# Moving a dense layer's row loads, row products and weight narrowing between queues and engines

## The chip, the cores and the metric

The kernel runs on one core of a Trainium2 chip. The metric is device time in microseconds (us) from one launch; it is read as the median of several runs. The engines are named as in the profile: PE is TensorE (matmuls), PEld its weight load, DVE is VectorE, ACT is ScalarE, POOL is GpSimd, SP is SyncE, which here only issues DMAs.

## What is computed

Three parts follow each other: attention with a bias that a small network makes of positions, a dense layer of two matrix products with a leaky activation, and a mixture of experts. Only the seam between the first two and the dense layer itself matter here. Cut to that:

```python
attn_out = attn @ v                      # softmax(q k^T / 8 + bias), 4 x 8 heads, 576 rows, 64 wide
x = attn_out.transpose(0, 2, 1, 3).reshape(2304, 512)
h = x @ w_in                             # 512 -> 2048
g = np.maximum(h, 0.0) + alpha * np.minimum(h, 0.0)
y = g @ w_out                            # 2048 -> 512; goes into the routing and the experts
```

## The kernel before, in words

**Attention** works through 16 pairs (two heads of one batch entry each) in rounds; an instruction list (ROUND) fixes the order, and nearly every instruction is pinned to it. Of each pair it writes the unnormalised output, transposed, to a DRAM tensor xT, and the inverse row sums to a DRAM tensor rs.

**The dense layer** cuts its 2304 rows into 6 blocks of 384 and the hidden width into 16 pieces f of 128. One step is one block and one f. A step's `up` is 12 matmuls of 384 columns that make h, then two ScalarE passes (L699, L701), one VectorE pass (L702) that makes g, a ScalarE pass that makes its high part gh (L709) and one that makes its low part gl (L711; GpSimd for block 0, VectorE for the others). Its `down` is 9 matmuls of 512 columns that add into three PSUM tiles ys. The loop issues `up` of step n+1 ahead of `down` of step n. Blocks 0 and 1 are interleaved and share their weights (steps n = 0 to 31: block 0's f and, two f behind, block 1's); blocks 2 to 5 follow one by one. All products use a high and a low part of each operand, so every operand passes through a cast to its high part on ScalarE and a subtraction for its low part.

**Weights.** The 16 pieces arrive as 64-bit numbers, 1 MB each (w_fetch, w_load: tile `wide`). `w_narrow` makes 32-bit ones of them by three VectorE passes (L649, L650, L651; tile `wr`), and then starts the load of piece f+2. `w_split` makes high and low parts (tiles w0h, w0l and so on, numbered on through the blocks: w16 is block 2's first, w32 block 3's, w48 block 4's); the low part L680 is VectorE's or GpSimd's by the list WL_DVE. Pieces 0 and 1 are narrowed in slices inside attention's fixed order. Piece 2 is fetched by a hook in the last full round but one of attention and narrowed by a call of w_narrow behind attention's code. `prep(n + 3)` does narrowing and splitting three steps ahead of use.

**Rows.** For a block's 384 rows, each of four column groups c needs xT's rows (tile xa, or xs for block 2) and rs spread over 64 partitions twice (tile rb): `x_load` issues three DMAs. Then VectorE multiplies the two (L587, `x_sum`), ScalarE casts to the high part (L592) and VectorE subtracts for the low part (L593). rb has one buffer, xa two. Blocks 0 and 1 go another way, inside attention (`x_early`, on GpSimd, L604 to L606). Block 2's rows are loaded and made in one go near the end of blocks 0 and 1, those of blocks 3 to 5 at f = 4, 6, 8 and 10 of the block before.

**Order.** A scheduler orders each engine's instructions by a simulated time in which transfers have a modelled duration; an instruction whose operands it takes to be ready may move ahead of others of its engine. `keep_in_program_order(i)` ties i behind the instruction of the same engine that was traced just before it, and to nothing else. Each engine, and SP's queue, runs its instructions strictly in the order that comes out.

**Routing.** When a block ends, its ys are copied out by ScalarE (L763) and VectorE (L764, tile y) and routed during the next block, a piece after each step; blocks 2 to 5 share one set of ys tiles.

## Time and profile before

| | |
|---|---|
| runs | 848.19, 850.45, 856.14 us; median 850.45 us |
| profiled execution | 855.61 us, of which the span from first to last instruction is 853.4 us |
| busy share of the span | PE 91%, PEld 76%, DVE 66%, ACT 57%, POOL 36% |
| chain that ended last | PE 42% of the span, DVE 3%, DMA 3%, ACT 2% |
| dense layer, about 319 to 778 us | PE busy but for short stretches; its granted clock is full (1.00) except behind some of them |

The busy share counts all time in which an instruction was in progress. An engine's clock is given as the share of full speed that was granted (1.00 is 2.4 GHz, 0.50 is 1.2 GHz); only PE's changes here. What costs time in a kernel with a PE this busy is read from stretches of 20 us: how much of each PE was idle, and how much it ran at the lower level.

### The profile page before, as it was taken

How to read it: one execution, taken by the hardware profiler on the slowest of the kernel's cores; microseconds unless marked ns; L12 is line 12 of the kernel's file. 1: busy time of each engine (PE TensorE's matmuls, PEld its weight loads, DVE VectorE, ACT ScalarE, POOL GpSimd, SP SyncE). 2: the span in 40 equal slices, each digit the busy share in tenths (PEclk: the TensorE clock that was granted, in tenths of full speed). 3: DMA queues.
4: the chain of work that ended last, by engine and by line, in shares of the span. 5: the costliest groups of instructions: out<-in, count | busy, mean ns of one | idle time of the engine just before them, and what ended most of it. 6: DMA issues, size and time to landing. Idle time of an engine off the chain costs nothing.

```text
span 853.4 us, 18376 instructions
## 1 busy us (share of the span) xinstructions
PE 780.0 (91%) x7428; PEld 647.7 (76%) x7428; DVE 561.1 (66%) x979; ACT 485.7 (57%) x961; POOL 304.8 (36%) x231
## 2 busy tenths in 40 slices
PE   5876599999999898999999999989989999998994
PEld 5766577777777667898998789879878899886332
DVE  8956668888888758897336665755666656465103
ACT  8742478888888744334446555646554656554002
POOL 6974325365564613114221431433233232131000
PEclk9989799999999999999999999999989999999897
DMA  6799895948742424553002000410010014337996
GB/s 204 183 211 194 192 243 174 249 119 233 239 133 85 143 91 164 197 201 119 2 1 65 10 1 1 160 38 1 1 28 1 1 58 154 109 104 263 391 379 222
DMA packets 59493, 114.44 MB, mean 134 GB/s; under 512 B 10640, under 2 KB 38160, under 8 KB 57360
## 3 DMA queue, kind: packets, MB, share of 16 engines
q1 hardware_dynamic: 59408, 113.26, 44.0%
q8 instruction: 58, 0.95, 0.5%
q14 instruction: 27, 0.22, 0.1%
HBM read 91.95 MB, written 21.29 MB: 133 GB/s over the span
## 4 chain that ended last, share of the span: by engine, by line
PE 42%; DVE 3%; DMA 3%; ACT 2%; issue 1%; POOL 0%; SPq 0%; DVEq 0%; ACTq 0%
PE ys L723 17%; PE h L691 16%; PE ops L1091 3%; DMA rb<-rs 2%; PE hps L1091 2%; DVE xa L587 1%; PE lp L783 1%; DMA xa<-xT 1%; PE turn L1100 0%; PE o L1118 0%; PE tl L830 0%; DVE g L702 0%; ACT g L699 0%; PE sp L842 0%; PE sp L843 0%
## 5 line engine op out<-in xcount | busy, mean ns | idle before, releaser
L702 DVE SCALAR_TENSOR_TENSOR g<-g,nal 128x384 f32<-128x384 f32 x96 | 87.7, 913 | 76.3 <-ACT g L701 75.8
L419 ACT ACTIVATE e<-z,m 128x576 f32<-128x576 f32 x144 | 109.9, 767 | 22.0 <-DVE m L399 22.0
L399 DVE CUSTOM_DVE_ANT_0 z<-s,nb 128x576 f32<-128x576 f32 x144 | 108.2, 755 | 18.7 <-PE s L381 11.0
L709 ACT ACTIVATE gr<-g 128x384 fp32r<-128x384 f32 x95 | 49.8, 524 | 113.1 <-DVE g L702 113.0
L467 PE MATMUL o<-g,v 128*64 128x256 f32 (+1 forms) x640 | 88.9, 424 | 4.1 <-DVE m L399 3.6
L455 ACT ACTIVATE g<-t 128x640 f32<-128x640 f32 x96 | 67.2, 702 | 34.7 <-PE t L439 30.7
L161 PE MATMUL acc<-wp,mask 128*128 128x64 bf16 (+1 forms) x1680 | 59.2, 201 | 22.1 <-issue 12.5
L161 PEld LDWEIGHTS <-mask 128*128 128x128 bf16 (+1 forms) x1680 | 57.0, 105 | 24.1 <-issue 14.7
L439 PE MATMUL t<-ident,e 64*128 64x64 f32 x1440 | 68.7, 224 | 5.8 <-DVE m L399 3.6
L711 DVE TENSOR_TENSOR gr<-g,gr 128x384 fp32r<-128x384 f32 x79 | 53.4, 676 | 31.4 <-ACT gr L709 29.7
L439 PEld LDWEIGHTS t<-ident,e 64*128 64x128 f32 x1440 | 66.2, 140 | 7.7 <-issue 5.4
L699 ACT ACTIVATE g<-h 128x384 f32<-128x384 f32 x96 | 46.7, 486 | 43.9 <-PE h L691 41.5
L467 PEld LDWEIGHTS o<-g,v 128*64 128x64 f32 x640 | 44.8, 141 | 34.0 <-DVE m L399 3.8
L381 PE MATMUL s<-kh,qh 64*128 64x288 f32 x320 | 62.0, 383 | 8.1 <-DVE rows L186 5.6
L142 ACT ACTIVATE mask<-pr,wb 128x576 bf16<-128x576 f16 (+4 forms) x81 | 47.0, 665 | 24.1 <-PE acc L161 24.1
L711 POOL TENSOR_TENSOR gr<-g,gr 128x384 fp32r<-128x384 f32 x16 | 20.0, 1250 | 93.2 <-ACT gr L709 78.4
L381 PE MATMUL s<-kh,ql 64*128 64x288 f32 x320 | 48.8, 299 | 0.0
L381 PE MATMUL s<-kl,qh 64*128 64x288 f32 x320 | 48.8, 300 | 0.0
L354 POOL TENSOR_SCALAR qh<-raw 128x1216 fp32r<-128x1216 f32 x16 | 19.4, 1210 | 80.2 <-PE s L381 75.5
L701 ACT ACTIVATE g<-h 128x384 f32<-128x384 f32 x96 | 46.6, 486 | 0.0
L381 PEld LDWEIGHTS s<-kh,qh 64*128 64x128 f32 x320 | 31.7, 193 | 17.2 <-issue 7.6
L356 POOL TENSOR_TENSOR ql<-raw,qh 128x1216 fp32r<-128x1216 f32 x16 | 44.7, 2793 | 0.0
(986 smaller groups left out, 2048.4 us busy)
## 6 DMA issues: line engine op xcount, KB each, us to landing
wide<-in_w_dram SPq DMA_DIRECT2D x16, 1024.0 KB
ep<-in_mw_dram SPq DMA_DIRECT2D x30, 512.0 KB
raw<-in_qk_dram SPq DMA_DIRECT2D x16, 896.0 KB
nb<-W SPq DMA_DIRECT2D x12, 576.0 KB
v<-in_v_l_dram SPq DMA_DIRECT2D x16, 320.0 KB
pre<-in_mw_dram SPq DMA_DIRECT2D x10, 512.0 KB
er<-in_mw_dram SPq DMA_DIRECT2D x9, 512.0 KB
em<-in_mw_dram SPq DMA_DIRECT2D x8, 512.0 KB
```

What stands on the lines that cost most here:

```text
L161: nc.tensor.matmul(dst[:, u // 8, :, :, 4 * (u % 8) : 4 * (u % 8) + 4], mask[:, (16 * k + u) % RING, cols], wp[:, part], start=part == 0, ...
L381: nc.tensor.matmul(s[:, hf, :288], st["q", a][d, o : o + P], st["k", b][d, 288 * h : 288 * h + 288], start=n_ == 0, stop=n_ == len(seq) - 1,),
L399: self.nc.vector.tensor_tensor_reduce(out=z.rearrange("p (a b) -> p a b", a=2), in0=s[:, :, :288], in1=self.nb[st["hp"]][:, slot].rearrang ...
L419: self.nc.scalar.activation(e, z, AF.Exp, bias=m, scale=-1.0, accum_out=st["sum"][:, slot : slot + 1]),
L439: self.pin(i, nc.tensor.transpose(tp[:, r, 64 * c : 64 * c + 64], e[q, k0 : k0 + P], self.ident[q, q]))
L455: self.pin(i, nc.scalar.activation(dst, src, AF.Copy))
L467: nc.tensor.matmul(op[64 * h : 64 * h + 64, 0, :n], st["v"][:, h, c], g[:, h, c], start=c == 0, stop=c == 4),
L691: nc.tensor.matmul(h, w_[:, c * P : (c + 1) * P], x_[:, c], start=c == 0 and n_ == 0, stop=c == NC - 1 and n_ == 2,)
L702: nc.vector.scalar_tensor_tensor(g, neg, self.nal[:, f : f + 1], g, ALU.mult, ALU.add)
L709: nc.scalar.activation(gh, g, AF.Copy)
L711: eng.tensor_tensor(gl, g, gh.bitcast(F32), ALU.subtract)
L723: i = self.nc.tensor.matmul(self.ys[blk][t], g_[:, t * P : (t + 1) * P], w_[:, 512:], start=f == 0 and n_ == 0, stop=f == NF - 1 and n_ == 2,)
```

## The change

Four edits, all in the dense layer and its seam with attention.

- **Rows of blocks 3 to 5**: loads stay at f = 4, 6, 8 and 10; product, cast and low part are traced one step later, at f = 5, 7, 9 and 11. Product and low part go to GpSimd, each tied behind the instruction traced before it on that engine. As rb has one buffer, the load of group c+1 follows the product of group c, and so stands two steps ahead of its own product.
- **Rows of block 2**: loads stay; product, cast and low part of groups 0 and 1 are traced one step later, of groups 2 and 3 two steps later. Products go to GpSimd, tied; low parts stay on VectorE, tied.
- **Narrowing**: the first of the three VectorE passes is tied behind the VectorE instruction traced before it; the other two depend on it. For piece 2 that puts it behind attention's last VectorE instruction.
- **Fetch of piece 2**: its hook moves from the eighth to the fourth transpose of the same round.

```diff
@@ class Moe
-    def x_sum(self, xu, rb):
-        self.nc.vector.tensor_tensor(xu, xu, rb, ALU.mult)
-
-    def x_split(self, blk, c, xu):
-        nc = self.nc
-        xh, xl = self.x[blk]
-        nc.scalar.activation(xh[:, c], xu, AF.Copy)
-        nc.vector.tensor_tensor(xl[:, c], xu, xh[:, c].bitcast(F32), ALU.subtract)
...
-    def x_make(self, blk, c, xu, rb):
-        self.x_sum(xu, rb)
-        self.x_split(blk, c, xu)
-
+    def x_make(self, blk, c, xu, rb, low):
+
+        nc = self.nc
+        xh, xl = self.x[blk]
+        self.tc.keep_in_program_order(nc.gpsimd.tensor_tensor(xu, xu, rb, ALU.mult))
+        nc.scalar.activation(xh[:, c], xu, AF.Copy)
+        self.tc.keep_in_program_order(low.tensor_tensor(xl[:, c], xu, xh[:, c].bitcast(F32), ALU.subtract))
...
@@ w_narrow
-        nc.vector.tensor_scalar(t, w[:, :, 1], 3, 0x3FFFFFFF, ALU.logical_shift_left, ALU.bitwise_and)
+        i = nc.vector.tensor_scalar(t, w[:, :, 1], 3, 0x3FFFFFFF, ALU.logical_shift_left, ALU.bitwise_and)
+        self.tc.keep_in_program_order(i)
...
@@ run
                 for c in range(NC):
                     self.x_load(2, c, *x2[c])
-                for c in range(NC):
-                    self.x_sum(*x2[c])
                 self.x_alloc(2)
-                for c in range(NC):
-                    self.x_split(2, c, x2[c][0])
+            for k in range(2):
+                if n + 1 < total and seq[n + 1] == (1, NF - 2 + k):
+                    for c in (2 * k, 2 * k + 1):
+                        self.x_make(2, c, *x2[c], nc.vector)
             if n < total - LATE_DOWN:
                 self.down(n, us.pop(n))
             elif n == total - 1:
                 break
-            if 2 <= blk < NBLK - 1 and 4 <= f < 12 and f % 2 == 0:
+            if 2 <= blk < NBLK - 1 and 4 <= f < 12:
                 c = (f - 4) // 2
-                if c == 0:
+                if f == 4:
                     self.x_alloc(blk + 1)
-                t3 = parts(c, blk + 1)
-                self.x_load(blk + 1, c, *t3)
-                self.x_make(blk + 1, c, *t3)
+                if f % 2 == 0:
+                    t3 = parts(c, blk + 1)
+                    self.x_load(blk + 1, c, *t3)
+                else:
+                    self.x_make(blk + 1, c, *t3, nc.gpsimd)
...
-        at(i - np_, 7, moe.w_fetch, f)
+        at(i - np_, 3 if f == 2 else 7, moe.w_fetch, f)
```

## Rows read from the trace of the kernel before

**Rows 1.** Busy time by stretch of 20 us (in brackets instructions), then PE's clock, DMA share, GB/s

```profile
core 0: us, PE busy (x) PEld busy (x) DVE busy (x) ACT busy (x) POOL busy (x), PEclk, DMA share, GB/s
280.00:300.00 20.00, 16.37 (x205) 11.77 (x201) 15.46 (x34) 13.17 (x29) 12.34 (x11) 0.86 0.42 133
...
340.00:360.00 20.00, 18.23 (x85) 15.95 (x84) 17.77 (x20) 6.55 (x14) 2.58 (x2) 0.91 0.58 200
...
400.00:420.00 20.00, 19.75 (x98) 17.75 (x99) 6.36 (x9) 9.72 (x19) 5.44 (x4) 1.00 0.01 2
...
460.00:480.00 20.00, 18.09 (x88) 15.27 (x87) 12.28 (x17) 11.19 (x21) 5.58 (x3) 0.91 0.15 48
...
560.00:580.00 20.00, 16.98 (x90) 15.38 (x90) 10.59 (x13) 7.98 (x14) 8.15 (x4) 0.91 0.08 20
...
620.00:640.00 20.00, 15.76 (x76) 14.00 (x75) 13.71 (x18) 11.10 (x22) 6.90 (x4) 0.83 0.11 30
```

**Rows 2.** PE's timeline: start, duration, instruction, in brackets idle time before and its releaser

```profile
295.79 4.53 PE L467 MATMUL o<-g,v 128*64 128x256 f32 x20 [3.63 <-DVE m L399]
...
355.67 0.53 PE L723 MATMUL ys<-w2h,gr 128*128 128x512 f32 x1 [1.77 <-ACT gr L709]
...
456.06 0.50 PE L691 MATMUL h<-x,w16h 128*128 128x384 f32 x2
...
471.74 0.60 PE L770 MATMUL ty_0th<-idr,y 128*128 128x128 f32 x4 [1.83 <-DVE y L764]
...
563.03 0.96 PE L723 MATMUL ys<-w34h,gr 128*128 128x512 f32 x3 [3.02 <-DVE gr L711]
...
633.26 0.80 PE L723 MATMUL ys<-w48h,gr 128*128 128x512 f32 x1 [4.24 <-DVE y L764]
```

**Rows 3.** DVE's timeline at the end of attention

```profile
287.69 1.42 DVE L641 SCALAR_TENSOR_TENSOR wr<-wide,wr 128x512 uint32<-128x512 uint32 x1
...
294.37 0.69 DVE L649 TENSOR_SCALAR wr<-wide 128x1024 uint32<-128x1024 uint32 x1 [3.24 <-DMA wide<-in_w_dram]
```

**Rows 4.** SP's timeline at the end of attention

```profile
289.13 0.33 SPq L623 DMA_DIRECT2D wide<-in_w_dram  x1
```

**Rows 5.** DVE's timeline in blocks 2 to 4

```profile
465.68 0.56 DVE L587 TENSOR_TENSOR xa<-xa,rb 128x384 f32<-128x384 f32 x1 [3.20 <-DMA rb<-rs]
...
469.93 0.56 DVE L587 TENSOR_TENSOR xa<-xa,rb 128x384 f32<-128x384 f32 x1 [1.19 <-DMA rb<-rs]
...
558.61 2.76 DVE L587 TENSOR_TENSOR xa<-xa,rb 128x384 f32<-128x384 f32 x1 [2.30 <-DMA rb<-rs]
...
619.74 2.11 DVE L702 SCALAR_TENSOR_TENSOR g<-g,nal 128x384 f32<-128x384 f32 x1 [1.15 <-ACT g L701]
...
630.03 2.57 DVE L587 TENSOR_TENSOR xa<-xa,rb 128x384 f32<-128x384 f32 x1 [2.07 <-DMA rb<-rs]
```

**Rows 6.** POOL's timeline in the dense layer

```profile
451.67 1.26 POOL L711 TENSOR_TENSOR gr<-g,gr 128x384 fp32r<-128x384 f32 x1 [8.20 <-ACT gr L709]
...
619.03 2.41 POOL L680 TENSOR_TENSOR w49l<-wr,w49h 128x1024 fp32r<-128x1024 f32 x1 [2.00 <-ACT w49h L678]
```

**Rows 7.** Groups by line, 318 to 790 us: busy us, mean ns of one

```profile
L702 DVE SCALAR_TENSOR_TENSOR g<-g,nal 128x384 f32<-128x384 f32 x96 | 87.7, 913 | 76.3 <-ACT g L701 75.8
L711 DVE TENSOR_TENSOR gr<-g,gr 128x384 fp32r<-128x384 f32 x79 | 53.4, 676 | 31.4 <-ACT gr L709 29.7 <-issue 1.3
...
L699 ACT ACTIVATE g<-h 128x384 f32<-128x384 f32 x96 | 46.7, 486 | 43.9 <-PE h L691 41.5 <-DVE gr L711 1.4 <-POOL gr L711 1.0
...
L651 DVE SCALAR_TENSOR_TENSOR wr<-wide,wr 128x1024 uint32<-128x1024 uint32 x13 | 18.0, 1388 | 0.1
```

**Rows 8.** Line 604's instructions: duration in ns, least, median, most

```profile
L604 POOL TENSOR_TENSOR xu<-xu,xb x8: 1004/1010/1531, 131.6 to 298.8; 128x384 f32<-128x384 f32 x8
```

**Rows 9.** The chain that ended last, 415 to 430 us: start, us, what

```profile
417.08 2.09 PE ys L723 x9
419.17 2.08 PE h L691 x12
```

**Rows 10.** ACT's timeline in block 2

```profile
461.79 1.04 ACT L678 ACTIVATE w18h<-wr 128x1024 fp32r<-128x1024 f32 x1
```

## Prediction

> **What bounds the kernel now.** I read three views, in this order. First the busy time in stretches of 20 us, to see where PE loses time at all [rows 1]. The stretch from 400 us is what a good one looks like: PE busy for 19.75 of 20 us at full clock. A step of the dense layer there is nine matmuls of a `down` and twelve of an `up`, 2.09 + 2.08 = 4.17 us [rows 9]. Five stretches fall short, and each loses twice: PE idles, and behind the idle time it runs for some microseconds at the lower of its two clocks, where a matmul takes twice as long. I count the idle time as 20 less the busy time, and the clock as 20 x (1 - PEclk).
>
> Second, PE's own timeline, for who ended each long idle time; third, the timelines of the engines so named. All five come down to one pattern: a VectorE instruction that waits for a DMA, or has work in front of it that waits for one, with everything behind it in VectorE's strict order, although that work was ready.
>
> At 291 us PE waits 3.63 us for attention's score pass [rows 2]. That pass stands in VectorE's queue behind the first narrowing pass of piece 2, which waited 3.24 us for its weights [rows 3]. These were asked for only at 289.13 [rows 4], just as the last slice of piece 1, which used the same buffer, ended at 289.11 [rows 3]. Nothing needs piece 2 before the dense layer; the scheduler took its weights as landed.
>
> At 471 us PE waits 1.83 us for a copy of ys, at 563 us 3.02 us for a low part of g, at 633 us 4.24 us for a copy of ys again [rows 2]. In front of these stand row products that waited 3.20 and 1.19 us, 2.30 us, and 2.07 us for the inverse sums rb [rows 5]. These products belong to the next block, or the one after; with one rb buffer each could ask for its sums only when the one before was done, and each was placed early. Two of them took 2.76 and 2.57 us in place of 0.56 [rows 5].
>
> At 355 us PE waits 1.77 us for a cast of g [rows 2]: VectorE is busy for 17.77 us of that stretch, but for 6.36 of the one from 400 us [rows 1]. It narrows weights far ahead of use, and g queues between.
>
> **The change, part by part.**
>
> *Narrowing of piece 2.* Its first pass is tied behind attention's last VectorE instruction, so it can't stand in front of a score pass. This returns 3.63 us of idle time and 20 x 0.14 = 2.8 us of clock [rows 1, 2]: **6.4 us**. The fetch three transposes earlier in its round gives nothing: the transfer still waits for the buffer until 289.11, and SP has little to hold back there. The three passes (0.69 us [rows 3] and two of at most 1.39 [rows 7]) now fall behind attention, 3.5 us, while PE has three `up` of pieces 0 and 1 (6.2 us by [rows 9]) to do; if that cover were gone they would cost up to 3.5.
>
> *Narrowing of the others.* Tied behind the low part of g of the step before, VectorE's work spreads. The idle time at 355 us goes, with its clock: 1.77 + 1.8 = **3.6 us** [rows 1]. The tie has its price. The piece's `up` comes two `up` and three `down` behind the `up` whose low part now precedes the narrowing: five half-steps, 10.4 us [rows 9]. Into these must go three ScalarE passes of 0.49, g 0.91 and its low part 0.68 [rows 7], narrowing 0.69 + 2 x 1.39 [rows 3, 7], a cast of 1.04 [rows 10] and, where GpSimd makes the weight's low part, 2.41 [rows 6]. That is 9.97 us, with 0.4 to spare; one more g in between, and it is 0.5 late. Five of the fourteen pieces have their low part on GpSimd, one of them piece 2. The others save about half of 2.41, and are in time. So the cost lies between 0 and 4 us (four pieces, 1 us each); I take 1.0, as PE has other matmuls to fill with. The load of piece f+2 follows the narrowing of f and then has two steps of 4.17 us twice over, 16.7 us, against some 5 us from 289.13 to 294.37 [rows 3, 4]: it isn't late.
>
> *Rows of blocks 3 to 5.* Twelve products and twelve low parts leave VectorE, and with them the waits for rb. This returns what PE lost at the three block boundaries, by [rows 1]: 1.91 + 1.8, 3.02 + 1.8 and 4.24 + 3.4, **16.2 us**. On GpSimd the product stands behind the weight's low part of the step, two steps (8.3 us) behind its load; the waits of 1 to 3 us above end inside that. If one doesn't, only weight low parts are queued behind it on GpSimd, made three steps ahead. ScalarE's cast, which isn't tied, may wait for the product with relus behind it; that is in the bounds below. Next late after the DMA waits is the copying out of ys at a boundary: blocks 2 to 5 share these tiles, so the first `down` waits for three copies whatever the change does. I leave 1.0 us of the boundaries unrecovered (0 to 3).
>
> *What GpSimd costs VectorE.* A product takes 1.01 us there [rows 8] against 0.56 [rows 5], hidden as GpSimd is idle for most of each stretch [rows 1]. What isn't hidden is that VectorE stands still: the g pass from 619.74 took 2.11 us and ended 0.4 us behind GpSimd's pass from 619.03 to 621.44 [rows 5, 6]. The mean g takes 0.91 and the mean low part 0.68 [rows 7], where a product of that size alone takes 0.56 [rows 5]: at most 96 x 0.35 + 79 x 0.12 = 43 us of delay, from 125 us of GpSimd work in the layer (43 weight low parts of 2.4, 16 low parts of g of 1.3 [rows 6]), 0.34 us for each. The 28 new passes (16 products, 12 low parts) of 1.01 us make 28 us, so 9.6 us of delay, in pieces of less than 1 us. On the path I take 1.5 us, with 0 and 9.6 as ends, as a step fills 4.17 us of PE and the path of a step's g 3 us (below).
>
> The Trainium skill speaks against this part: "GPSIMD Engine Reference", section "Engine selection", gives plain elementwise work to VectorE, as GpSimd takes about twice as long with two inputs. "SBUF — State Buffer" (section "SBUF: two separate sides") adds that the two share a port pair as an exclusive lock. The rows agree with both; counted as that lock at its worst, all 28 us would come back as cost and the gain would be near nothing, which is rival 1 at its end.
>
> *Rows of block 2.* Their products move from VectorE, where they were placed early, to GpSimd behind the low part of g that starts at 451.67 [rows 6]; four of 1.01 us end at about 457. The low parts of groups 2 and 3 stand behind g's low part of the last step before block 2, 3.05 us behind that `up` (three ScalarE passes of 0.49, g 0.91, low part 0.68 [rows 7]), and end 1.1 us later at 4.2, with up to 1 us more if a GpSimd pass is in the way. Block 2's first `up`, which began at 456.06 [rows 2], follows one `down` and wants the last of them at its tenth matmul, 2.09 + 1.7 = 3.8 us behind [rows 9]. So 0.4 to 1.4 us late, unless PE does the next `down` first; with copies of ys on VectorE in between it could be 4. I take 1.0 (0 to 4).
>
> **The sum.** Gains 6.4 + 3.6 + 16.2 = 26.2 us; costs 1.0 + 1.0 + 1.5 + 1.0 = 4.5; net 21.7. The profiled execution took 855.61 us, 5.2 above the median; the order of instructions that causes the stalls is the same in each execution, so the difference holds for both: 855.61 - 21.7 = 833.9 for such an execution, and 850.45 - 21.7 = **828.8 us** as the forecast for the median.
>
> **Rivals.** *1. GpSimd holds VectorE on the path.* For: 0.3 us of delay for each us already. Against: it moves short pieces, and a step has slack. At 9.6 us of delay in place of 1.5, and as much again for the clock, it costs 16.2 more: 845. If all 28 us came onto the path, the time would be 828.8 - 1.5 + 28 = 855, no measurable gain. *2. The stalls only change place.* The change would not do what it says: boundaries stay as the copying of ys, not the DMA wait, ends them. For: PE's releaser at 471 and 633 is that copy. Against: in all three places the DMA wait stands right before it. With half of 16.2 kept as loss: 837. *3. Slower: weights late.* If the tied narrowing misses its `up` by 1.8 us, which it does once the 10 us above become more than 12.2, each of 13 pieces costs what the stall at 355 us did, 3.6 us: 47 - 26 = 21 us, 871. Against: two thirds of the pieces have a margin above 1 us, and PE can do other matmuls.
>
> **How the numbers follow.** Forecast 0.73, rival 1 (845 to 855) 0.12, rival 2 0.10, rival 3 0.05. With all costs at zero the time would be 824, and single runs before lie 2 below to 6 above their median: low end 817. The costs at their upper ends (boundaries 3, late weights 4, GpSimd 9.6, block 2's rows 4: 20.6 in place of 4.5) would give 845; few will be there at once, and 842 leaves out rivals 1 and 3, 0.17. Within 1% (8.5 us) is about what a measurement can't tell from no change. Forecast, rival 2 and a little of rival 1 make 0.85 for faster; the most of rival 1 makes 0.10 for the same; rival 3, 0.05 for slower.
>
> **What would show it.** Right: no wait for `wide` on VectorE inside attention and PE busy at full clock to its end; no row product on VectorE in the layer; the three boundaries with PE idle below 1 us and clock 1.00; products on GpSimd that don't wait for rb. Wrong: GpSimd waiting for rb with weight low parts behind it, PE released by a weight's low part in blocks 0 and 1, long ScalarE waits for products, or g passes of 1.5 us and more ahead of most of PE's idle time.

## The result, and the profile after

The changed kernel took 828.66 us, the median of four runs (827.0 to 830.02), against 850.42 for the kernel before, run four times beside it (848.19 to 856.14). The ratio is 0.9734 [0.9691, 0.9778], so the change returns 21.8 us. The forecast was 828.8. One of the twelve runs of e4 below (944.56 us, at a mean granted clock of 0.745 where the others have 0.96 to 0.97) is slow and not counted.

The head of the profile page after, whose profiled execution took 829.09 us:

```profile
span 827.3 us, 18364 instructions
PE 769.7 (93%) x7428; PEld 639.3 (77%) x7428; DVE 552.8 (67%) x951; ACT 487.3 (59%) x961; POOL 339.6 (41%) x259
...
PE 82%; DVE 7%; issue 4%; ACT 2%; DMA 2%; POOL 2%; DVEq 0%; ACTq 0%; SPq 0%; POOLq 0%
```

The last line is the chain of work that ended last: PE makes 82% of it. The 42% of the kernel before can't be set beside it, as the shares of that chain add up to only half of its span. VectorE issues 28 instructions fewer than before (979) and GpSimd 28 more (231): the 16 products and 12 low parts that moved.

The stretches of 20 us that fell short before [rows 1], and three more, in the view by stretch of the kernel after (columns as in [rows 1]):

```profile
280.00:300.00 20.00, 20.00 (x299) 15.92 (x297) 17.05 (x41) 17.37 (x39) 11.95 (x12) 1.00 0.43 139
300.00:320.00 20.00, 18.52 (x163) 14.08 (x159) 9.56 (x18) 8.80 (x20) 6.18 (x10) 1.00 0.39 140
...
340.00:360.00 20.00, 20.00 (x102) 17.99 (x101) 15.92 (x19) 8.90 (x19) 3.05 (x3) 1.00 0.30 106
...
380.00:400.00 20.00, 18.70 (x92) 16.24 (x91) 14.51 (x14) 7.85 (x15) 7.14 (x4) 1.00 0.35 122
...
440.00:460.00 20.00, 18.72 (x106) 16.38 (x105) 18.40 (x22) 14.84 (x29) 9.61 (x6) 1.00 0.00 1
460.00:480.00 20.00, 20.00 (x116) 17.79 (x114) 9.19 (x13) 11.61 (x20) 10.43 (x5) 1.00 0.00 1
...
560.00:580.00 20.00, 20.00 (x106) 17.01 (x105) 12.62 (x21) 12.01 (x24) 10.38 (x7) 1.00 0.13 40
...
620.00:640.00 20.00, 20.00 (x119) 18.15 (x118) 11.24 (x16) 12.65 (x24) 7.65 (x4) 1.00 0.08 21
```

The five stretches in which PE lost time before are now full, at the full one of its two clocks. I add up, for all stretches from 280 to 740 us and for both kernels, idle time as 20 less the busy time and clock as 20 x (1 - PEclk), as the prediction did. Before it is 19.4 + 12.2 = 31.6 us; after, 4.4 + 0.0. These 27.2 us are close to what the spans differ by, 853.4 - 827.3 = 26.1 us. They are not quite the same thing: of the 26.1, 1.8 lie ahead of the attention work that is compared below, in a part that the change doesn't touch, and 1.2 are lost again early in that attention work, so that some 25.5 lie where the sum counts. The 4.4 us that are left lie almost all in three stretches: 1.48 us from 300, 1.30 from 380 and 1.28 from 440. The first is the end of attention, with waits of 0.48 and 0.86 us that the kernel before has too (0.48 and 1.31). Who ended the last two is in PE's timeline after (in brackets the idle time and its releaser):

```profile
388.66 0.62 PE L686 MATMUL h<-x,w10h 128*128 128x384 f32 x2 [1.02 <-ACT g L696]
389.56 0.44 PE L686 MATMUL h<-x,w10l 128*128 128x384 f32 x1 [0.27 <-POOL w10l L675]
...
447.89 0.44 PE L686 MATMUL h<-x,w16h 128*128 128x384 f32 x1 [0.87 <-DVE x L605]
...
452.73 0.44 PE L686 MATMUL h<-x,w16h 128*128 128x384 f32 x1 [0.41 <-DVE x L605]
```

The first two are the `up` of piece 10. Only the second of them, 0.27 us, is a weight that comes too late: the low part w10l, which GpSimd makes. The first, 1.02 us, ends with a ScalarE pass over an earlier `up`. ScalarE's timeline after:

```profile
383.86 0.49 ACT L694 ACTIVATE g<-h 128x384 f32<-128x384 f32 x1 [3.49 <-PE h L686]
386.01 1.06 ACT L673 ACTIVATE w10h<-wr 128x1024 fp32r<-128x1024 f32 x1 [1.66 <-DVE wr L646]
387.74 0.49 ACT L694 ACTIVATE g<-h 128x384 f32<-128x384 f32 x1 [0.67 <-PE h L686]
388.12 0.48 ACT L696 ACTIVATE g<-h 128x384 f32<-128x384 f32 x1
```

There are two h tiles. The first pass over one of them starts at 383.86; the second pass over it, at 388.12, stands in ScalarE's order behind the cast w10h, which waits for the narrowing, and behind the first pass over the next h, which waits for PE. PE runs out of work at 387.64, when w10h is already there (387.07), and waits for that h tile. So it is the order on ScalarE that costs the 1.02 us. The last two of PE's waits are the low parts of block 2's rows. The prediction named costs at both places, the first for another reason.

One figure needs care. The two profiled executions differ by 855.61 - 829.09 = 26.5 us and the medians by 21.8. The profiled execution of before was one of its longest; more of this at the end.

### The profile page after: what moved, and what is told of

It is laid out like the page before. It is cut to its first block, busy times and chain, and to the rows that moved or that the text cites. A ratio compares the mean times of both kernels' runs of the same rounds, so it can differ in the third digit from the quotient of the medians.

```text
span 827.3 us, 18364 instructions
## 1 busy us (share of the span) xinstructions
PE 769.7 (93%) x7428; PEld 639.3 (77%) x7428; DVE 552.8 (67%) x951; ACT 487.3 (59%) x961; POOL 339.6 (41%) x259
## 4 chain that ended last, share of the span: by engine, by line
PE 82%; DVE 7%; issue 4%; ACT 2%; DMA 2%; POOL 2%; DVEq 0%; ACTq 0%; SPq 0%; POOLq 0%
PE h L686 23%; PE ys L718 22%; PE o L467 10%; PE s L381 8%; PE acc L161 5%; PE t L439 5%; PE ops L1087 3%; PE hps L1087 2%; DVE mask L145 1%; DVE z L399 1%; PE lp L778 1%; DMA W<-rows 1%; DVE r L485 1%; PE turn L1096 0%; DVE x L605 0%
## 5 line engine op out<-in xcount | busy, mean ns | idle before, releaser
L697 DVE SCALAR_TENSOR_TENSOR g<-g,nal 128x384 f32<-128x384 f32 x96 | 99.6, 1038 | 83.1 <-ACT g L696 82.9
L354 POOL TENSOR_SCALAR qh<-raw 128x1216 fp32r<-128x1216 f32 x16 | 19.4, 1214 | 79.7 <-PE s L381 75.6
```

The lines of the kernel that those rows point to most:

```text
L697: nc.vector.scalar_tensor_tensor(g, neg, self.nal[:, f : f + 1], g, ALU.mult, ALU.add)
```

## Experiments

Lines in the tables and diffs are those of each kernel. Times are medians. A "phase" is measured on PE's timeline: A from the first transposition of row sums in attention (114 to 118 us into the span) to the first `up` of the dense layer, B from there to the first `down` of piece 32 (block 3's first), C and D the next two blocks. "Loss" is idle time plus clock from 280 to 740 us, as above. The kernel before stands twice; its second look (e13) is a single run. e1 to e4 ran on one chip, e5 to e8 on another and e10 to e13 on a third, each time beside runs of the kernel before, whose medians were 847.23, 848.87 and 849.32 us; ratios therefore compare better than times. e1, e3 and e4 were run twelve times, the others six.

| kernel | us | ratio to before | A | B | C | D | loss |
|---|---|---|---|---|---|---|---|
| before | 850.42 | | 200.8 | 231.9 | 82.3 | 76.3 | 31.6 |
| before, looked at again | 849.75 | | 200.95 | 231.5 | 80.1 | 76.1 | 28.5 |
| after | 828.66 | 0.9734 [0.9691, 0.9778] | 195.2 | 224.9 | 73.6 | 73.2 | 4.4 |
| e1 ties alone | 841.55 | 0.9935 [0.991, 0.996] | 194.5 | 231.5 | 79.0 | 74.8 | 16.3 |
| e4 tie of piece 2 alone | 843.29 | 0.9944 [0.9915, 0.9972] | 194.05 | 233.8 | 81.55 | 75.7 | 26.7 |
| e2 rows of 3 to 5 alone | 833.35 | 0.9835 [0.9797, 0.9874] | 201.0 | 224.6 | 73.4 | 73.85 | 12.8 |
| e3 rows of 2 alone | 851.83 | 1.0049 [1.002, 1.0077] | 199.9 | 230.9 | 81.7 | 74.9 | 25.1 |
| e8 fetch hook back | 826.55 | 0.975 [0.9716, 0.9785] | 194.4 | 224.9 | 73.6 | 73.2 | 4.7 |
| e5 rows 3 to 5 on VectorE | 826.06 | 0.9749 [0.9713, 0.9784] | 193.4 | 224.9 | 73.45 | 73.5 | 4.5 |
| e7 GpSimd, not tied | 836.07 | 0.9875 [0.9831, 0.9918] | 193.3 | 233.35 | 72.8 | 74.6 | 14.4 |
| e6 low parts four times | 834.95 | 0.9852 [0.9818, 0.9887] | 195.5 | 224.9 | 78.6 | 77.2 | 11.4 |
| e12 only piece 2 tied | 826.55 | 0.975 [0.9709, 0.9791] | 193.8 | 225.2 | 73.6 | 73.2 | 5.5 |
| e11 block 2's rows as before | 828.6 | 0.9774 [0.9736, 0.9813] | 193.3 | 225.4 | 73.4 | 73.8 | 5.6 |
| e10 block 2's products earlier | 825.38 | 0.9734 [0.9698, 0.9771] | 194.5 | 225.1 | 73.6 | 73.2 | 5.0 |

**e1: the narrowing ties alone**, on the kernel before.

```diff
-        nc.vector.tensor_scalar(t, w[:, :, 1], 3, ...)
+        i = nc.vector.tensor_scalar(t, w[:, :, 1], 3, ...)
+        self.tc.keep_in_program_order(i)
```

> The kernel before with the ties on the first narrowing pass of every piece, and nothing else. My theory (each part returns the stall that its own waits cause): attention's stall of 6.4 us and the one of 3.6 us at 355 us go, late weights cost 1.0 to 1.3, so about 9 us below the kernel before, 841.5 us; the three boundaries keep their idle time of 1.9, 3.0 and 4.2 us. Rival (the row products hold VectorE up and narrowing merely stands beside them): under 3 us below, as the products that wait for rb behind attention are still there.

Measured: 841.55, 5.5 us below the median of the kernel before on that chip by the ratio (0.65% of 847). Phase A is 6.4 us shorter, just the attention term. The stall at 355 us is gone too. The gain lies between the 9 us of the theory and the 3 of the rival: phase B is as long as before, and C and D are about 1 us shorter each than e13's. The boundaries were to keep 1.9, 3.0 and 4.2 us of idle time; they have 2.57, 3.74 and 1.41. PE's timeline of e1 at the first two:

```profile
464.22 0.45 PE L692 MATMUL h<-x,w19l 128*128 128x384 f32 x1 [2.57 <-DVE w19l L681]
...
555.19 0.69 PE L692 MATMUL h<-x,w36l 128*128 128x384 f32 x1 [3.74 <-DVE w36l L681]
```

and VectorE's timeline of e1 shows what stood ahead of the first:

```profile
460.27 0.56 DVE L587 TENSOR_TENSOR xa<-xa,rb 128x384 f32<-128x384 f32 x1 [1.16 <-DMA rb<-rs]
460.75 3.42 DVE L681 TENSOR_TENSOR w19l<-wr,w19h 128x1024 fp32r<-128x1024 f32 x1
```

The row products that wait for rb are still on VectorE; what the ties push later meets them. The low part w19l behind the product took 3.42 us in place of 1.2, beside GpSimd's w20l (460.73 to 463.09 us), which adds to it; w36l, 3.36 us beside w38l, is the same at the next boundary. So behind attention, in phase B, the ties' gain isn't seen while the rows stay where they were.

**e4: the tie of piece 2 alone**, on the kernel before.

```diff
+        if f == 2:
+            self.tc.keep_in_program_order(i)
```

> The kernel before with the tie on the first narrowing pass of piece 2 alone. My theory: attention's stall goes, 6.4 us below the kernel before, 844 us, and the stall of the dense layer near 355 us stays. Rival (the wait for the weights only moves behind attention): within 2 us of the kernel before.

Measured: 843.29, ratio 0.9944 [0.9915, 0.9972]. Phase A falls by 6.75 us, B rises by 1.9. The attention term is there; of it, a part is lost again in blocks 0 and 1, where the boundary at 460 us lost 2.81 + 3.4 in this execution. The other half of the theory missed: the stretch from 340 us is full, and PE idles at other places, for 1.33 us at 390 and, right behind attention, for piece 2 itself:

```profile
321.48 0.44 PE L693 MATMUL h<-x,w2l 128*128 128x384 f32 x1 [2.37 <-POOL w2l L682]
```

Between the narrowing passes of piece 2, now behind attention, stands a row product of block 3 that waits 2.14 us for rb (it starts at 312.00 us). The cover that the prediction counted on is gone then, which by its sum costs up to 3.5 us. Part of the 2.4 seen comes from w2l itself, which took 4.71 us in place of 2.4. In the changed kernel no such product stands there.

**e2: rows of blocks 3 to 5 alone.** Loads two steps ahead, products and low parts tied on GpSimd; nothing of the rest.

```diff
-            if 2 <= blk < NBLK - 1 and 4 <= f < 12 and f % 2 == 0:
+            if 2 <= blk < NBLK - 1 and 4 <= f < 12:
...
-                t3 = parts(c, blk + 1)
-                self.x_load(blk + 1, c, *t3)
-                self.x_make(blk + 1, c, *t3)
+                if f % 2 == 0:
+                    t3 = parts(c, blk + 1)
+                    self.x_load(blk + 1, c, *t3)
+                else:
+                    self.x_make(blk + 1, c, *t3, nc.gpsimd)
```

> The kernel before with only the rows of blocks 3 to 5 changed: product, cast and low part one step later, product and low part tied and on GpSimd. My theory: the three boundaries' 16.2 us come back less 1.0 to 2.5 us, so 13.7 to 15.2 us below the kernel before, about 836 us, with attention's stall of 3.6 us still there. Rival (stalls change place, ys copies end the boundaries): half of it, about 842.5 us.

Measured: 833.35, ratio 0.9835 [0.9797, 0.9874], 14.0 us. This is the largest part. The view by stretch of e2:

```profile
280.00:300.00 20.00, 16.77 (x219) 12.63 (x215) 14.93 (x35) 12.12 (x26) 12.09 (x13) 0.83 0.38 122
...
340.00:360.00 20.00, 18.31 (x92) 16.23 (x91) 17.98 (x20) 8.21 (x16) 4.12 (x3) 1.00 0.60 221
...
540.00:560.00 20.00, 20.00 (x121) 17.73 (x120) 10.24 (x12) 11.96 (x22) 9.16 (x4) 1.00 0.00 1
```

Beside the same stretches of the kernel before, looked at again (e13):

```profile
280.00:300.00 20.00, 16.68 (x213) 12.52 (x211) 14.63 (x33) 11.98 (x26) 12.79 (x15) 0.83 0.36 111
...
340.00:360.00 20.00, 18.22 (x84) 15.79 (x83) 17.36 (x21) 7.69 (x16) 2.75 (x2) 0.91 0.62 216
...
540.00:560.00 20.00, 17.78 (x104) 15.55 (x102) 16.44 (x22) 11.94 (x24) 7.91 (x3) 1.00 0.47 163
```

The attention stretch is untouched, 3.23 us idle at clock 0.83. The boundary that e13 has in the stretch from 540 us, with 2.22 us idle, is full in e2, and so are the other two. Phase B is 6.9 us shorter than e13's: 3.8 of it the boundary at 460 us (2.02 + 1.8 in e13), most of the rest between 320 and 400 us, in the first steps of the layer, though rows of blocks 3 to 5 aren't needed there. The reason stands behind the narrowing term below.

**e3: rows of block 2 alone.** Products on GpSimd and low parts one and two steps before block 2; blocks 3 to 5 as before.

```diff
-                for c in range(NC):
-                    self.x_sum(*x2[c])
...
-                for c in range(NC):
-                    self.x_split(2, c, x2[c][0])
+            for k in range(2):
+                if n + 1 < total and seq[n + 1] == (1, NF - 2 + k):
+                    for c in (2 * k, 2 * k + 1):
+                        self.x_make(2, c, *x2[c], nc.vector)
```

> The kernel before with only the rows of block 2 changed: products later, tied and on GpSimd, low parts tied on VectorE. My theory: nothing was to gain here and 0.4 to 1.4 us are lost where block 2's first matmuls wait for the low parts, so 0 to 1.5 us above the kernel before. Rival (VectorE's work on these rows is part of what made the dense layer's first steps slow): 2 to 4 us below.

Measured: 851.83, ratio 1.0049 [1.002, 1.0077], 4.2 us slower and more than either theory gave. Its trace doesn't show where. Its loss, 25.1 us, is below that of both looks at the kernel before (31.6 and 28.5), and A to D are no longer than e13's in sum (587.4 against 588.65). What is longer lies outside these phases: 116.65 against 114.6 us ahead of them, 76.0 against 75.5 behind the layer's last `down`. Nothing that this edit touches is there, and the parts ahead vary by as much between all these kernels (113.7 to 118.2). Nor can these two profiles show 4.2 us: they are of runs of 850.65 us, below e3's median, and 849.75, above the 847.23 of the kernel before on e3's chip. The size of this part by itself stays open; e11 below asks for it in the changed kernel.

**e8: the fetch hook back to the eighth transpose** (7, counted from 0), in the changed kernel.

```diff
-        at(i - np_, 3 if f == 2 else 7, moe.w_fetch, f)
+        at(i - np_, 7, moe.w_fetch, f)
```

> The changed kernel with the fetch of piece 2 back at the eighth transpose. My theory: nothing, within 1 us, since the transfer waits for the same buffer in either place. Rival (the earlier fetch is part of the gain): 2 us or more above the changed kernel.

Measured: 826.55, and loss and phases are the changed kernel's within 0.8 us. The earlier hook gives nothing that can be measured, and the traces say why: in the changed kernel SP issues this load at 287.90 us, right behind the last slice of piece 1, which ends at 287.87; in e8 these are 285.52 and 285.49, as in [rows 3, 4]. On that chip e8 stands for the changed kernel in what follows.

**e5: rows of blocks 3 to 5 on VectorE**, in the changed kernel, at the same tied places.

```diff
-        self.tc.keep_in_program_order(nc.gpsimd.tensor_tensor(xu, xu, rb, ALU.mult))
+        self.tc.keep_in_program_order((first or nc.gpsimd).tensor_tensor(xu, xu, rb, ALU.mult))
...
-                    self.x_make(blk + 1, c, *t3, nc.gpsimd)
+                    self.x_make(blk + 1, c, *t3, nc.vector, nc.vector)
```

> The changed kernel with the rows of blocks 3 to 5 made one step later and tied as there, but product and low part on VectorE. My theory (place in the order decides, not the engine): within 2.5 us of the changed kernel, 826.5 to 831 us, no idle PE at the boundaries. Rival (GpSimd is what frees VectorE): waits of VectorE for rb come back, and 5 us or more are lost.

Measured: 826.06 against 826.55 of e8: the same. The groups by line of e5 on VectorE, 300 to 770 us:

```profile
L697 DVE SCALAR_TENSOR_TENSOR g<-g,nal 128x384 f32<-128x384 f32 x96 | 91.6, 954 | 69.2 <-ACT g L696 69.1
...
L603 DVE TENSOR_TENSOR xa<-xa,rb 128x384 f32<-128x384 f32 x12 | 6.6, 551 | 0.0
```

Twelve products on VectorE, each 0.55 us, and no idle time ahead of any: with the load two steps ahead and the product held at its place, the sums have landed. At these places the engine doesn't matter. The four products of block 2 stay on GpSimd in this run, so it says nothing of them.

**e7: GpSimd without the places.** Products, and low parts of blocks 3 to 5, on GpSimd at the old places, untied; the narrowing tied as in e1.

```diff
-        self.nc.vector.tensor_tensor(xu, xu, rb, ALU.mult)
+        self.nc.gpsimd.tensor_tensor(xu, xu, rb, ALU.mult)
...
+        low = nc.gpsimd if blk > 2 else nc.vector
...
-        nc.vector.tensor_tensor(xl[:, c], xu, xh[:, c].bitcast(F32), ALU.subtract)
+        low.tensor_tensor(xl[:, c], xu, xh[:, c].bitcast(F32), ALU.subtract)
```

> The kernel before with the narrowing ties, and with all row products and the low parts of blocks 3 to 5 on GpSimd, at the places in the program that they had before and without ties. My theory (place decides): products stand early in GpSimd's queue, wait for rb there with weight low parts behind them, and PE loses part of it: 4 to 12 us above the changed kernel. Rival (the engine decides): within 2 us of the changed kernel, as VectorE no longer waits.

Measured: 836.07, 9.5 us above e8. GpSimd's waits from 300 to 460 us (us in total, times, longest):

```profile
POOL xa L587 <- DMA rb<-rs: 15.3, 3, 8.9
...
POOL xs L587 <- DVE wr L652: 5.9, 1, 5.9
```

PE's two longest waits:

```profile
406.90 0.74 PE L725 MATMUL ys<-w11h,gr 128*128 128x512 f32 x1 [2.41 <-ACT gr L711]
...
437.34 0.45 PE L693 MATMUL h<-x,w15l 128*128 128x384 f32 x1 [2.99 <-POOL w15l L682]
```

and GpSimd's timeline ahead of the second:

```profile
429.49 1.99 POOL L587 TENSOR_TENSOR xs<-xs 128x384 f32<-128x384 f32 x1 [5.91 <-DVE wr L652]
...
433.67 1.01 POOL L587 TENSOR_TENSOR xs<-xs 128x384 f32<-128x384 f32 x1 [0.93 <-DMA xs<-rs]
434.62 2.66 POOL L682 TENSOR_TENSOR w15l<-wr,w15h 128x1024 fp32r<-128x1024 f32 x1
```

The waits moved to GpSimd with the products, and once it is as my theory has it: the weight low part w15l stands behind three products of block 2 that waited for a narrowing pass and for rs, and PE waits 2.99 us for it. The rest is another mechanism. The longest wait for rb, 8.9 us, ends at 305.74 us, ahead of the layer, and no long wait of PE ends with what is queued behind it. The wait of 2.41 us has no row product near it: a g pass took 2.43 us, from 403.86, beside GpSimd's w12l (403.52 to 405.88). So the time came out inside my range, and its cause is the theory's in part only. In phases C and D e7 is as good as the changed kernel (147.4 against 146.8 in sum). So the engine alone is worth part of the gain and the places the rest.

**e6: the low parts of blocks 3 to 5 four times**, 36 more GpSimd passes in the changed kernel.

```diff
-        self.tc.keep_in_program_order(low.tensor_tensor(xl[:, c], ...))
+        for _ in range(4 if low is nc.gpsimd else 1):
+            self.tc.keep_in_program_order(low.tensor_tensor(xl[:, c], ...))
```

> The changed kernel with each of the twelve low parts on GpSimd made four times over, the same values each time: 36 more passes of 1.0 us on GpSimd. By the forecast's 1.5 us for 28 passes: 1.9 us above the changed kernel. By rival 1 with delay at the rate of the kernel before, 0.34 us for each us: 12 us above; with all of it on the path: 36 us.

Measured: 834.95, 8.4 us above e8, 0.23 us for each pass. It lies nearer the rival's 12 than the forecast's 1.9. Where it is lost, in GpSimd's timeline of e6:

```profile
592.57 5.58 POOL L606 TENSOR_TENSOR x<-xa,x 128x384 fp32r<-128x384 f32 x4 [0.64 <-ACT x L604]
598.12 2.36 POOL L676 TENSOR_TENSOR w48l<-wr,w48h 128x1024 fp32r<-128x1024 f32 x1
```

VectorE's at the same moment:

```profile
598.29 2.61 DVE L698 SCALAR_TENSOR_TENSOR g<-g,nal 128x384 f32<-128x384 f32 x1 [1.01 <-ACT g L697]
```

and PE's:

```profile
601.51 0.50 PE L719 MATMUL ys<-w46h,gr 128*128 128x512 f32 x1 [1.98 <-ACT gr L705]
```

Four passes in a row take 5.58 us and push w48l to 598.12; the g pass that starts beside it takes 2.61 us in place of 0.62 and ends 0.4 us behind it, and PE waits 1.98. The 0.23 us are a mean: against e8 the trace loses in two places only, 4.5 us from 580 to 620 and 2.6 from 660. So GpSimd does hold VectorE on the path, as rival 1 had it, once passes are piled up ahead of a weight low part. One pass at a time, as the change has it for blocks 3 to 5, doesn't (e5).

**e12: only piece 2 tied**, in the changed kernel; the other thirteen pieces' narrowing left to the scheduler.

```diff
-        self.tc.keep_in_program_order(i)
+        if f == 2:
+            self.tc.keep_in_program_order(i)
```

> The changed kernel with the tie on narrowing for piece 2 alone. By the forecast's sum the stall of 3.6 us near 355 us comes back and the late weights' 1.3 us go: 2.3 us above the changed kernel, a ratio to the kernel before of 0.9775. Rival (without row products on VectorE at the start of the dense layer, early narrowing no longer stalls it): within 1 us, or below.

Measured: 826.55, on another chip than e8 but with the same ratio, 0.975. My theory wanted 2.3 us more, which these intervals can't tell from nothing. The trace can: the stall of 3.6 us isn't back. The view by stretch of e12:

```profile
340.00:360.00 20.00, 19.40 (x96) 17.05 (x96) 19.21 (x23) 8.24 (x17) 3.47 (x2) 1.00 0.63 215
360.00:380.00 20.00, 18.97 (x96) 16.96 (x96) 19.63 (x20) 7.95 (x16) 6.66 (x4) 1.00 0.56 194
```

Without the ties VectorE is packed from 340 to 380 us (19.21 and 19.63 us of 20; 15.92 in the changed kernel's first of these) and PE loses 0.60 and 1.03, and another 1.20 at 319 us, all three waiting for a cast of g. But the 1.30 us of the changed kernel from 380 us aren't there, and 0.84 in place of 1.28 from 440. In sum e12 loses 5.5 us and the changed kernel 4.4 to 4.7: the ties trade one for the other.

**e11: block 2's rows as before**, in the changed kernel.

```diff
+                for c in range(NC):
+                    self.x_sum(*x2[c])
...
-                        self.x_make(2, c, *x2[c], nc.vector)
+                for c in range(NC):
+                    self.x_split(2, c, x2[c][0])
```

> The changed kernel with block 2's rows as in the kernel before: products early and untied on VectorE, low parts untied. By the forecast's sum this part costs 1.0 us, and 1.3 us of idle PE show it, so 1.3 us below the changed kernel, a ratio to the kernel before of 0.973. Rival (the parts don't add: VectorE has tied narrowing now, and early products fall between): 1 us or more above the changed kernel, 0.976 or more.

Measured: 828.6, ratio 0.9774 [0.9736, 0.9813] against e12's 0.975 [0.9709, 0.9791] on the same chip. The intervals overlap and the loss is 5.6 against 5.5: inconclusive. The trace has 0.53 us from 440 in place of the changed kernel's 1.28, and 1.28 from 420 where that has none. If moving block 2's rows is worth anything, it is some 2 us, not clear of the noise.

**e10: block 2's loads two steps and products two to three steps earlier**, and the low part of piece 10 on VectorE (the pair (0, 10) added to WL_DVE), in the changed kernel.

```diff
-            if n + 1 < total and seq[n + 1] == (0, NF - 1):
+            if n + 1 < total and seq[n + 1] == (0, NF - 2):
...
+            if n + 1 < total and seq[n + 1] == (1, NF - 3):
+                for c in range(NC):
+                    self.tc.keep_in_program_order(nc.gpsimd.tensor_tensor(x2[c][0], x2[c][0], x2[c][1], ALU.mult))
```

> The changed kernel with two edits at the places where its PE still idles: block 2's row loads two steps and products one step earlier, and the low part of weight piece 10 on VectorE in place of GpSimd. My theory (each idle stretch is what its releaser shows): the 1.3 us at block 2's first matmuls and some of the 1.3 us at piece 10 go, 1 to 2.5 us below the changed kernel, which makes a ratio to the kernel before of 0.972. Rival (something else is late next): within 1 us of the changed kernel, 0.975.

Measured: 825.38, ratio 0.9734 [0.9698, 0.9771]; 1.2 us below e12, which stands for the changed kernel on that chip, and inside the interval. At piece 10 only the 0.27 us are gone; the 1.02 that wait for ScalarE stay, though GpSimd makes no low part there. The stretch from 440 us, where PE waited for block 2's low parts, loses only 0.22, but the one before it now loses 1.64 us, 0.62 of it for w15l, a weight low part of GpSimd:

```profile
420.00:440.00 20.00, 18.36 (x92) 16.04 (x92) 11.63 (x12) 9.95 (x19) 10.90 (x7) 1.00 0.25 78
```

Something else is late next, of about the same size. At 5 us of loss in 460 there is little left to gain here by this count.

**e13: the kernel before, looked at again**, unchanged.

> The kernel before once more, for a second look at how its stalls vary. Theory (the stalls are waits for transfers, so their length varies, not their place): the same five idle places, the sum of idle time and clock between 18 and 30 us. Rival (the order fixes their size too): within 2 us of 26.2.

Measured: 849.75 us, and a loss of 28.5 us, 18.1 idle and 10.4 of clock; the five places make 24.0 of it, against 26.2 in the first look. That is inside the theory's range and 0.2 us outside the rival's, so two looks hardly decide. The same five places lose, in lengths of their own: the boundary of blocks 2 and 3 lost 3.02 + 1.8 in the first look [rows 1] and 2.22 without a drop of the clock in this one.

## Why the prediction was right, and which steps were not

**Attention and piece 2: 6.4 us. Right.** Phase A fell by 5.6 in the changed kernel, and by 6.3 to 7.4 in e1, e4, e5 and e8; the changed kernel lost 1.2 us early in A, where nothing was changed. The stretch from 280 us went from 16.37 us busy at clock 0.86 [rows 1] to 20.00 at 1.00. The narrowing behind attention is covered, as forecast: VectorE's timeline after has the first pass right behind attention's last copy, and PE has no wait beside it once the layer has begun. Without the row products gone from there the cover fails, as e4 shows.

```profile
311.20 0.27 DVE L492 COPY rt<-o 9x128 f32<-9x128 f32 x1
311.39 0.67 DVE L643 TENSOR_SCALAR wr<-wide 128x1024 uint32<-128x1024 uint32 x1
```

**The fetch hook: nothing. Right**, by e8 and by SP's timeline.

**Rows of blocks 3 to 5: 16.2 us at the boundaries, 1.0 not recovered. Right in place and cause, nearly in size.** All three boundaries are full in the profile after, so nothing was left unrecovered. C and D fell by 8.7 and 3.1 us against the profiled execution of before and by 6.5 and 2.9 against e13. Taken alone (e2) the edit returned 14.0 in the median. The copies of ys that PE's waits named at 471 and 633 us [rows 2] were not the cause: nothing about them was changed, and those waits are gone. This was rival 2, and it falls. Why it works is sharper than I had it: I gave the gain to the engine and the earlier load alike, and e5 shows that VectorE does as well at the same places, e7 that GpSimd at the old places takes the waits along: in C and D without harm to PE, in B with some.

**Narrowing of the other pieces returns 3.6. Right in cause; what the ties return in the whole change is less.** The stall at 355 us is what the forecast took it for, and a wait for a transfer is in it too. This is VectorE's timeline of the kernel before; PE waits for the cast behind the second g pass:

```profile
347.21 0.69 DVE L649 TENSOR_SCALAR wr<-wide 128x1024 uint32<-128x1024 uint32 x1 [1.87 <-DMA wide<-in_w_dram]
347.81 0.61 DVE L702 SCALAR_TENSOR_TENSOR g<-g,nal 128x384 f32<-128x384 f32 x1
...
354.45 0.61 DVE L702 SCALAR_TENSOR_TENSOR g<-g,nal 128x384 f32<-128x384 f32 x1
```

The first g pass stands behind a narrowing pass that waits for its weights, the second behind four more narrowing passes and a weight low part. The ties alone take this stall away (e1). But with the rows moved, the time is the same within the noise whether all pieces are tied or piece 2 alone (e12): in idle time the ties then take 2.8 us (1.20, 0.60 and 1.03) and give back 1.3 at piece 10 and 0.4 at block 2. The 1.8 us of clock in the term come and go: in e2, without ties, the stall is still there, 1.69 us behind a wait of 1.62 for the weights, at full clock.

**Left out: two products of block 3 at the start of the layer.** This is VectorE's timeline of the kernel before in its second look (e13):

```profile
313.07 0.56 DVE L587 TENSOR_TENSOR xa<-xa,rb 128x384 f32<-128x384 f32 x1 [3.31 <-DMA rb<-rs]
...
317.53 0.56 DVE L587 TENSOR_TENSOR xa<-xa,rb 128x384 f32<-128x384 f32 x1 [0.98 <-DMA rb<-rs]
```

The tile is xa, so these are rows of a later block than 2: the scheduler had placed block 3's first two products some 140 us ahead of the others (the next one starts at 452.51). In e2 they are gone, and from 306 to 336 us that is all that its VectorE order differs in from e13's. PE's idle time from 320 to 340 us falls from 1.98 (2.37 in the first look) to 0.42, while the stall behind it stays. So these early waits cost about 1.5 to 2 us there, which the sum didn't have, and they weren't what made the stall at 355 us.

**Late weights: 1.0 us. Right in size, mostly not for the reason given.** The forecast had it in the four pieces whose low part GpSimd makes. It is one of them, piece 10, with 1.02 + 0.27 = 1.29 us, but only the 0.27 go when VectorE makes that low part (e10). The 1.02 are the order on ScalarE shown above, a cast and a pass that wait, with a pass behind them that PE needs; the prediction had no such term for it. Both come with the ties: e1 has them, e12 and the kernel before don't (e7, tied as well, has 0.76 us at piece 11 instead). Rival 3 falls with it.

**GpSimd on the path: 1.5 us of at most 9.6. Right in the size of the delay; on the path at one place only.** The groups by line of the kernel after, 300 to 770 us, first VectorE's, then GpSimd's:

```profile
L697 DVE SCALAR_TENSOR_TENSOR g<-g,nal 128x384 f32<-128x384 f32 x96 | 99.6, 1038 | 83.1 <-ACT g L696 82.9
...
L605 POOL TENSOR_TENSOR x<-xa,x 128x384 fp32r<-128x384 f32 x12 | 15.9, 1323 | 14.1 <-ACT x L604 14.1
L603 POOL TENSOR_TENSOR xa<-xa,rb 128x384 f32<-128x384 f32 x12 | 15.1, 1256 | 0.5 <-DMA rb<-rs 0.5
L603 POOL TENSOR_TENSOR xs<-xs 128x384 f32<-128x384 f32 x4 | 5.9, 1500 | 0.0
```

The mean g pass rose from 0.913 [rows 7] (0.900 in e13) to 1.038 us, 96 x 0.125 = 12 us of delay; with the rows of blocks 3 to 5 on VectorE (e5) it is 0.954, so 8 of the 12 go with these 24 GpSimd passes. All 28 took 36.9 us, not the 28 that I had from [rows 8]. The upper end of 9.6 was thus about the true size of the delay, and yet the time is the same without the 24 (e5): what they delay is off the path. e6 shows the point from which that ends.

Block 2's four products are another matter; e5 leaves them on GpSimd. GpSimd's and VectorE's timelines after:

```profile
441.54 5.88 POOL L603 TENSOR_TENSOR xs<-xs 128x384 f32<-128x384 f32 x4
...
446.47 1.83 DVE L605 TENSOR_TENSOR x<-xs,x 128x384 fp32r<-128x384 f32 x2
```

Beside them VectorE's low part of g took 1.37 us (0.56 elsewhere), its g pass 1.38 (0.61) and two low parts of block 2's rows 1.83 (1.01 in the kernel before), and PE's wait of 0.87 us ends with these. The wait of 0.41 us ends with two low parts that took 2.65, from 450.49, beside GpSimd's w18l (449.51 to 452.26). With the products earlier (e10), 0.22 us are left of the 1.28 there. So here a VectorE that GpSimd holds up does lie on the path; the forecast had this as the "up to 1 us more" in its term for block 2.

The Trainium skill's "GPSIMD Engine Reference", section "Engine selection", which gives plain elementwise work to VectorE, agrees with the durations, 1.26 us on GpSimd against 0.55 on VectorE (e5). By the time of the kernel the choice made no difference for the rows of blocks 3 to 5.

**Rows of block 2: 1.0 us of cost. Right:** 0.87 + 0.41 = 1.28 us of PE's idle time, released by these low parts. Against that stands what the old places cost, and e3 and e11 don't settle the balance.

**The parts don't add up.** e1, e2 and e3 alone gave -5.5, -14.0 and +4.2, together -15.3; the whole change gave -21.8. The three intervals together leave some 5 us of room in that sum, so the gap of 6.5 lies about at their edge. e1 shows one reason for it: the ties' gain is lost again to the row products while these stay. The 4.2 us of e3 are not explained.

**"The difference holds for both" was wrong.** The order of instructions is the same in each execution, but the waits are for transfers, and these differ in length: 31.6 and 28.5 us of loss in two looks at one kernel. The profiled execution of before was a long one. On it the account of loss closes: the five places returned 26.2 us, the stretches from 300 to 340 us, which I had left out as small, another 3.4 (1.92 + 0.6 and 2.37 before, 1.48 and nothing after), and 2.6 were lost at the two new waits; 27.0 of the 27.2 found. The second look has 3.1 us less to return, and from it to the changed kernel phases A to D fall by 21.7, as much as the median. So the hit to 0.2 us is in part luck. The sum of 21.7 was made for an execution that in fact gained 26.5: it left out the 3.4 us from 300 to 340, and its costs were some 2 us too large (1.5 for GpSimd on the path and 1.0 for the boundaries, of which nothing was seen beyond the waits that are left, and 0.6 too little for these). It was then carried over to a median that had about 5 us less to gain, and the two errors met.

## What to carry to other kernels

When an engine with a strict order waits for a transfer, look for the waiting instruction and hold it at a place where its data has landed. Which engine runs it came second here: moved to another engine at the old place, it took its wait along, and what that cost hung on what was queued behind it. When several stalls have one cause, credit each edit only with what a run of it alone, and one of the whole without it, return. Look at the whole order of an engine for instructions that a scheduler has moved far ahead: the two products at 313 us belonged to a block that began at about 540. Take a second profile of the kernel before ahead of any sum that is made against one execution, if the stalls are waits for transfers.

## What the runs showed of the hardware that was not expected

- Waits for small transfers vary from one execution to the next: in the two looks at the kernel before, the same product waited 2.30 and 1.53 us for rb at one boundary, and 1.69 and 0.98 at the start of the layer. The kernel before took from 842.03 to 852.57 us in eleven runs, and on the same chip e8, in which no such wait is on the path, from 825.04 to 827.91 in six. That the waits make this spread isn't shown: e3 keeps most of them and took from 849.04 to 853.52 in twelve runs.
- An idle time of the same length sometimes has a drop of PE's clock behind it and sometimes not. From 340 us, 1.77 and 1.78 us of idle time in the two looks at the kernel before left the granted clock of the stretch at 0.91, and 1.69 us in e2 at 1.00; yet 2.57 us in e1 left its stretch at 1.00 too, while 2.41 us in e7 cost 1.8 us. About half of what such an idle time costs hangs on this, and no run here shows what decides it.
- GpSimd's products took 1.26 us in the layer against 1.01 ahead of it [rows 8]. Of the low parts, 36 more, piled four in a row, cost 0.23 us each in the mean; one at a time they cost nothing that can be measured.
